# Block attention and a top-1 mixture of experts: k and q loaded one token a partition, one transposing transfer for each half

## The chip, the cores and the metric

The kernel runs on one core of a Trainium2 chip. The core has five engines, each with its own queue of instructions that it works off in order: PE (TensorE, the matrix multiplier, whose weight loads are listed apart as PEld), DVE (VectorE), ACT (ScalarE), POOL (GpSimd) and SP (SyncE, which here only issues transfers). Transfers run on 16 DMA engines. The metric is the device time of one execution in microseconds (us); lower is better.

## The reference

Eight batches of eight heads, 576 tokens each, 64 channels a head. Attention is causal by blocks of 64 tokens, and its output goes through a mixture of experts in which each token takes the one expert with the largest gate:

```python
scores = scale * np.matmul(q, k.transpose(0, 1, 3, 2))
mask = (pos[:, None] // 64) >= (pos[None, :] // 64)
scores = np.where(mask, scores, -1e9)
attn = np.exp(scores - scores.max(-1, keepdims=True))
attn = attn / (attn.sum(-1, keepdims=True) + 1e-9)
x = (attn @ v)                       # to (4608 tokens, 512)
logits = x @ w_gate                  # 8 experts
e_idx = np.argmax(logits, axis=1)
h = np.maximum(x[mask] @ w1[e], 0)   # 512 -> 1024, for the tokens of expert e
out[mask] = gate_w * sigmoid(x @ w_output_gate)[e] * (h @ w2[e])
```

Inputs and output are float32.

## The kernel before, in words

**Attention.** The 64 heads are taken two at a time: 32 pairs, each a `Pair` object. Products are made in 16-bit halves: a float32 operand is split into a high half (`ACT`, line 116) and the rest, a low half (`POOL`, line 117). For q and k both halves must stand with the 64 channels on the partitions, so they are turned. A pair goes through these steps:

- `fetch` (L104, L107) loads k and q of both heads into `nat`. The 576 tokens are one block of 64 (the "odd" block, L107) and four blocks of 128 (L104). In L104 partition p gets the four tokens 4p to 4p+3, which lie together in memory. Three `nat` buffers.
- `split` (L116, L117) writes the halves into `sp0` (high) and `sp1` (low), [128 partitions, 9 blocks, 128]. Two buffers of each.
- `turn` (L125, L127) is called once for `sp0` and once for `sp1`. Each time it issues five transposing transfers on SP: one of the odd block into `to`, and four of 32 partitions by 1024 columns into `tr`.
- `max_tile` (L165 to L197) multiplies q by k for the row maxima, `turn_max` (L206, L208) turns these, `prob_tile` (L222, L252) makes the products again, transposed, and takes the exponential on ACT into `pc` and `pcr`.
- `fetch_v`, `split_v` (L146, L150, L154, L155) load v with ten transfers into one of two buffers and split it. `values_odd` and `values` (L265 to L293) make the output, divide it and write it to `x_d` in memory with five transfers (L308, L311).
- `turn_x` and `finish_batch` (L318 and the lines from 475 on), after every fourth pair, make the gate of a batch and put its tokens into a table.

Since partition p holds tokens 4p to 4p+3, the order of tokens on the partitions is a mixed one (t, i), and v, the masks and `x_d` follow it: their patterns are "(i t) -> t i".

**Order of the work.** `round_of(g)` writes out the order of PE by hand: 139 rounds, four to a pair, in which several pairs are at different steps. Pair p takes its maxima in rounds 4p to 4p+2, its exponentials from 4p+5 on, its values in 4p+11 and 4p+12. The other engines get the order in which a scheduler places the same program's instructions; what has been placed on an engine is then worked off in that order. `turn` of pair p is written down at rounds 4p-7 and 4p-6, `split` at 4p-9 and 4p-8, `fetch` at 4p-12.

Products rotate through three PSUM buffers (`banks()`, `ps_s`): PE may fill one again when ACT or DVE have read it.

**Mixture of experts.** The last rounds overlap with the first tiles of the experts. After them come 22 steps; a step loads up to 4 MB of weights, splits them and multiplies (L763 to L924); each step's tokens are turned with one transposing transfer of 1024 or 2048 columns (`turned`, L854). The change leaves this part alone.

Of the kernel before, what the change touches and what calls it, by code (L numbers as in the profile page):

```python
# [8 lines left out]
F16 = mybir.dt.float16  # L9
# [5 lines left out]
ALU = mybir.AluOpType  # L15
# [5 lines left out]
P = 128  # L21
# [5 lines left out]
def block_attention_top1_moe(  # L27
# [11 lines left out]
    nc = tc.nc  # L39
    B, H, S, D = q.shape  # L40
# [5 lines left out]
    R0 = 64  # L46
# [3 lines left out]
    NR = 2 * S // P  # L50
    BIG = 60000.0
# [23 lines left out]
    sb = tc.alloc_tile_pool(name="sb", bufs=2)  # L75
# [16 lines left out]
    class Pair:  # L92


        def __init__(self, p):
            self.p = p
            self.b, self.hp = divmod(p, NP)
            self.tr, self.to = {}, {}

        def fetch(self):  # L100
            h0 = 2 * self.hp
            self.nat = ld.tile([P, 2, 2, 5, D], F32, name="nat", bufs=3)
            for w, src in enumerate((k, q)):
                nc.sync.dma_start(  # L104
                    self.nat[:, w, :, 1:5], src[self.b, h0:h0 + 2, R0:S].rearrange("h (p t) d -> p h t d", t=4)
                )
                nc.sync.dma_start(  # L107
                    self.nat[64 * w:64 * w + 64, 0, :, 0], src[self.b, h0:h0 + 2, 0:R0].rearrange("h p d -> p h d")
                )
            self.sp = [ld.tile([P, NR, P], F16, name=f"sp{c}", bufs=2) for c in range(2)]  # L110
# [6 lines left out]
                last_lo[0] = lo.tensor_tensor(sl[:, h], nat, sh[:, h], ALU.subtract)  # L117

        def room(self, c):
            self.tr[c] = sb.tile([P, 4, 2, P], F16, name=f"tr{c}", bufs=4)  # L120
            self.to[c] = sb.tile([P, P], F16, name=f"to{c}", bufs=4)

        def turn(self, c):
            self.room(c)
            nc.sync.dma_start_transpose(self.to[c], self.sp[c][:, 0])  # L125
            for n in range(4):
                nc.sync.dma_start_transpose(  # L127
                    self.tr[c][:, n].rearrange("c w (t i) -> c (w t) i", t=4),
                    self.sp[c][32 * n:32 * n + 32, 1:NR].rearrange("p r c -> p (r c)"),
                )  # L130

        def keys(self, c, ab, lo, hi):
            return self.tr[c][64 * ab:64 * ab + 64, lo:hi, 0]

        def asks(self, c, ab, lo, hi):
            return self.tr[c][64 * ab:64 * ab + 64, lo:hi, 1]

        def odd(self, c, ab, c0, c1):
            return self.to[c][64 * ab:64 * ab + 64, c0:c1]

        def fetch_v(self):
            h0 = 2 * self.hp
            self.vn, self.vh, self.vl = vns[self.p % 2], vhs[self.p % 2], vls[self.p % 2]
            for h in range(2):
                for n in range(4):
                    nc.sync.dma_start(  # L146
                        self.vn[:, 2 * n + h, 0:D],
                        v[self.b, h0 + h, R0 + P * n:R0 + P * n + P].rearrange("(i t) d -> t i d", t=4),
                    )
                nc.sync.dma_start(self.vn[64 * h:64 * h + 64, 8, 0:D], v[self.b, h0 + h, 0:R0])  # L150

        def split_v(self):
# [4 lines left out]
        def max_tile(self, i):  # L157
# [3 lines left out]
            def products(os, n, c0):  # L161
                m = P * (n + 1)
                main = [o[:, c0:c0 + m].rearrange("p (n x) -> p n x", x=P) for o in os]
                for ab in range(2):
                    nc.tensor.matmul(main[ab], self.asks(0, ab, n, n + 1)[:, 0], self.keys(0, ab, 0, n + 1), start=True, stop=False)  # L165
                for ab in range(2):
                    half = slice(64 * ab, 64 * ab + 64)
                    nc.tensor.matmul(  # L168
                        main[ab][:, n].rearrange("p (t i) -> p t i", t=4)[:, :, 16:32], mq[half], mk[half].rearrange("p (t x) -> p t x", t=4), start=False, stop=True
                    )  # L170
                for ab in range(2):
                    nc.tensor.matmul(
                        os[ab][:, c0 + m:c0 + m + R0], self.asks(0, ab, n, n + 1)[:, 0], self.odd(0, ab, 0, R0), start=True, stop=True
                    )

            if i < 2:
                ps = banks()
# [104 lines left out]
        def values(self, ab):  # L282
            for t in range(4):
                o = self.region(t)[:, ab]
                for c in range(t + 1):
                    i, c0 = ((1, 0), (0, 0), (2, 0), (0, 384))[c]
# [17 lines left out]
                self.xn.rearrange("p t (h d) -> p h t d", h=2), o[:, :, :, 0:D], sm.unsqueeze(3).broadcast_to([P, 2, NT, D]), ALU.mult  # L304
            )
            to = x_d[self.b * S:(self.b + 1) * S, self.hp * P:(self.hp + 1) * P]
            for n in range(4):
                nc.sync.dma_start(  # L308
                    to[R0 + P * n:R0 + P * n + P].rearrange("(i t) c -> t i c", t=4), self.xn[:, n]
                )  # L310
            nc.sync.dma_start(to[0:R0], self.xn[64:128, 4])  # L311

        def turn_x(self):
# [13 lines left out]
    with tc.high_priority(offset=3000):  # L327
# [12 lines left out]
        idg = const.tile([P, B, NT, 2], I32, name="idg")  # L340
# [13 lines left out]
    def masks():  # L354
# [10 lines left out]
        nc.vector.tensor_tensor(prt[:, 0:1], prt[:, 0:1], prt[:, 1:2], ALU.add)  # L365
        nc.vector.tensor_scalar(prt[:, 1:2], prt[:, 0:1], 31.5, -32.0, ALU.is_ge, ALU.mult)
        nc.vector.tensor_tensor(prt[:, 2:3], prt[:, 0:1], prt[:, 1:2], ALU.add)
        nc.vector.tensor_scalar(prt[:, 3:4], prt[:, 2:3], 15.5, BIG, ALU.is_le, ALU.mult)
        nc.vector.tensor_scalar(prt[:, 4:5], prt[:, 2:3], 15.5, None, ALU.is_ge)
        nc.vector.tensor_scalar(prt[:, 5:6], prt[:, 1:2], -1.0 / 16, None, ALU.mult)  # L370
        nc.vector.tensor_tensor(prt[:, 4:5], prt[:, 4:5], prt[:, 5:6], ALU.add)
        nc.vector.tensor_scalar(
            kext[:, 0:4], blk.unsqueeze(2).broadcast_to([P, 4, P]), prt[:, 4:5], -BIG, ALU.is_equal, ALU.mult
        )
        nc.vector.memset(kext[:, 0:4].rearrange("p n (t i) -> p n t i", t=4)[:, :, :, 0:16], 0.0)
        nc.vector.memset(kext[:, 4], 0.0)
        for a in (0, 64):
            nc.vector.memset(kext[a:a + 1], MS)
# [6 lines left out]
                )  # L385
        nc.gpsimd.memset(mk, BIG)
        nc.gpsimd.memset(mq, 0.0)
        nc.gpsimd.memset(mq.rearrange("p (t x) -> p t x", t=4)[:, :, 0:16], -BIG)

    def opening():  # L390


        x = Pair(0)
        y = Pair(1)
        x.fetch()
        y.fetch()
        x.split(0, nc.vector.tensor_copy, nc.vector)
        x.split(1, nc.scalar.copy, nc.gpsimd)
        rest = ps_v.tile([P, 2, 512], F32, name="ps_v")[:, 0].rearrange("p (a n) -> p a n", n=P)
        for i in range(2):  # L400
            x.room(i)
            ps = banks().rearrange("p a (b n) -> p (a b) n", n=P)
            for r in range(NR):
                nc.tensor.matmul(
                    ps[:, r - 1] if r else rest[:, i], x.sp[i][:, r], ident16, start=True, stop=True
                )
            to = x.tr[i].rearrange("c n w (t i) -> c w t n i", t=4)
            for w, cp in enumerate((nc.vector.tensor_copy, nc.scalar.copy)):
                for t in range(4):
                    cp(to[:, w, t], ps[:, 4 * w + t].rearrange("c (n i) -> c n i", n=4))  # L410
            nc.vector.tensor_copy(x.to[i], rest[:, i])
        y.split(0, nc.vector.tensor_copy, nc.gpsimd)
        y.split(1, nc.scalar.copy, nc.gpsimd)
        return x, y
# [4 lines left out]
    with tc.high_priority(offset=1000):  # L419
# [19 lines left out]
        nc.vector.tensor_scalar(t64, tcol, 64.0, None, ALU.mult)  # L439


        for t in range(4):
            nc.gpsimd.iota(idg[32 * t:32 * t + 32, :, 0:4, 0], pattern=[[S, B], [P, 4]], base=R0 + t, channel_multiplier=4)
        nc.gpsimd.iota(idg[:, :, 4, 0], pattern=[[S, B]], base=-R0, channel_multiplier=1)


# [520 lines left out]
    for p in range(1, NPR):  # L967
        base = 4 * p
# [191 lines left out]
```

## Time and profile before

| what | value |
|---|---|
| median of 3 runs | 1238.41 us (1229.64 to 1240.27) |
| the profiled execution's own time | 1231.79 us |
| its span, first to last instruction | 1230.1 us |
| busy in the span: PE, DVE, ACT, POOL | 66%, 44%, 37%, 28% |
| mean granted clock of PE | 0.805 of full speed |
| transfers issued by SP for attention | 918 |

The span has two parts. Up to about 765 us the pairs run, at a granted clock that is mostly 0.66 to 0.74, with PE busy half of the time; from 800 us on PE is busy for 0.89 to 0.96 of the time and the clock is at 0.93 to 0.99. A row of the timeline gives the start and the duration of an instruction (of several alike: of the group), engine and line, operation, destination and source; in brackets the idle time of the engine before it and what ended it. SP's rows have the time in which its queue was held by the issue of a transfer, waits included; the transfer itself comes after.

### The profile page before, as it was taken

How to read it: one execution, taken by the hardware profiler on the slowest of the kernel's cores; microseconds unless marked ns; L12 is line 12 of the kernel's file. 1: busy time of each engine (PE TensorE's matmuls, PEld its weight loads, DVE VectorE, ACT ScalarE, POOL GpSimd, SP SyncE). 2: the span in 40 equal slices, each digit the busy share in tenths (PEclk: the TensorE clock that was granted, in tenths of full speed). 3: DMA queues.
4: the chain of work that ended last, by engine and by line, in shares of the span. 5: the costliest groups of instructions: out<-in, count | busy, mean ns of one | idle time of the engine just before them, and what ended most of it. 6: DMA issues, size and time to landing. Idle time of an engine off the chain costs nothing. (4 is left out here: it accounts for less than half of the span.)

```text
span 1230.1 us, 23287 instructions
## 1 busy us (share of the span) xinstructions
PE 814.0 (66%) x8912; PEld 576.6 (47%) x8912; DVE 544.8 (44%) x928; ACT 457.6 (37%) x706; POOL 338.9 (28%) x392
## 2 busy tenths in 40 slices
PE   2155346455536553555535658689899999999996
PEld 1143234333324442344323436466667667667763
DVE  6032323232323332333223336524867768667741
ACT  2122223222222222322223223431766767657632
POOL 5122112311311231132131331544542232232101
PEclk9866767676666767667676778879999999999998
DMA  4232222332322332232332222624697999998141
GB/s 115 61 78 73 67 72 69 74 78 75 69 75 67 81 80 70 67 66 70 83 67 68 57 53 52 191 49 157 200 305 240 306 314 317 268 261 194 48 164 37
DMA packets 234920, 148.80 MB, mean 121 GB/s; under 512 B 172240, under 2 KB 207088, under 8 KB 234800
## 3 DMA queue, kind: packets, MB, share of 16 engines
q1 hardware_dynamic: 226752, 127.93, 38.7%
q0 software_dynamic: 8048, 19.29, 5.2%
q8 instruction: 72, 1.18, 0.4%
q14 instruction: 48, 0.39, 0.1%
HBM read 126.03 MB, written 19.34 MB: 118 GB/s over the span
## 5 line engine op out<-in xcount | busy, mean ns | idle before, releaser
L165 PE MATMUL ps_s<-tr 64*128 64x384 f16 (+3 forms) x256 | 54.2, 351 | 263.1 <-ACT pc L252 236.7
L256 DVE TENSOR_TENSOR lpc<-pc 128x512 f16<-128x512 f32 (+1 forms) x64 | 49.7, 776 | 377.4 <-ACT pc L252 377.4
L117 POOL TENSOR_TENSOR sp<-nat,sp 128x320 f16<-128x320 f32 (+1 forms) x126 | 90.3, 745 | 446.8 <-DMA tr<-sp 328.8
L886 PEld LDWEIGHTS <-w1b 128*128 128x128 f16 (+1 forms) x2208 | 176.6, 98 | 28.4 <-issue 5.1
L886 PE MATMUL ps_s<-xt,w1b 128*128 128x256 f16 (+5 forms) x1920 | 176.0, 253 | 2.9 <-DVE w1b L765 1.2
L116 ACT CAST sp<-nat 128x256 f16<-128x256 f32 (+1 forms) x124 | 45.1, 427 | 337.1 <-DMA tr<-sp 240.2
L915 PE MATMUL ps_o<-w2b,hh 128*128 128x512 f16 (+1 forms) x560 | 166.6, 379 | 1.7 <-ACT hh L894 1.4
L765 DVE TENSOR_TENSOR w2b<-w2f,w2b 128x1024 bf16<-128x1024 f32 x80 | 92.6, 1219 | 91.3 <-ACT w2b L763 90.0
L168 PEld LDWEIGHTS <-mq 64*128 64x128 f16 x256 | 13.4, 101 | 246.0 <-issue 245.9
L190 DVE TENSOR_REDUCE nmx<-ps_s 128x2 f32<-128x896 f32 (+3 forms) x128 | 82.1, 682 | 73.5 <-PE ps_s L182 67.3
L293 PE MATMUL ps_v<-vn,pc 128*128 128x65 f32 x512 | 109.7, 332 | 0.0
L915 PE MATMUL ps_o<-w2b,hl 128*128 128x512 f16 x280 | 106.1, 379 | 0.1
L765 DVE TENSOR_TENSOR w1b<-w1f,w1b 128x1024 bf16<-128x1024 f32 x80 | 93.0, 1217 | 3.7 <-ACT w1b L763 3.4
L293 PEld LDWEIGHTS ps_v<-vn,pc 128*128 128x128 f32 x512 | 88.9, 231 | 4.0
L924 POOL DMA_INDIRECT out_dram<-ys,ids x38 | 46.0, 1212 | 158.4 <-ACT ys L923 94.1
L252 ACT ACTIVATE pc<-ps_s 128x1024 f32<-128x1024 f32 (+1 forms) x96 | 82.1, 875 | 17.7 <-PE ps_s L222 17.0
L915 PEld LDWEIGHTS <-hh 128*128 128x128 f16 x560 | 54.2, 98 | 63.3 <-ACT hh L894 1.5
L763 ACT CAST w1b<-w1f 128x1024 f16<-128x1024 f32 x80 | 78.3, 1046 | 5.3 <-DMA w1f<-in_moe_w_dram 5.3
L763 ACT CAST w2b<-w2f 128x1024 f16<-128x1024 f32 x80 | 77.5, 1043 | 0.0
L222 PE MATMUL ps_s<-tr 64*128 64x384 f16 (+3 forms) x256 | 43.9, 337 | 42.4 <-ACT qe L208 18.3
L222 PE MATMUL ps_s<-tr,tr 64*128 64x512 f16 (+3 forms) x512 | 67.8, 344 | 3.9 <-issue 3.7
L318 PE MATMUL ps_s<-ident,xn 128*128 128x128 f32 x160 | 39.8, 410 | 45.2 <-ACT pc L252 42.2
(214 smaller groups left out, 1613.4 us busy)
## 6 DMA issues: line engine op xcount, KB each, us to landing
w1f<-in_moe_w_dram SPq DMA_DIRECT2D x80, 512.0 KB
w2f<-in_moe_w_dram SPq DMA_DIRECT2D x80, 512.0 KB
nat<-in_k_dram SPq DMA_DIRECT2D x32, 256.0 KB
nat<-in_q_dram SPq DMA_DIRECT2D x32, 256.0 KB
vn<-in_v_dram SPq DMA_DIRECT2D x256, 32.0 KB
x_d<-xn SPq DMA_DIRECT2D x128, 64.0 KB
tr<-sp SPq DMA_TRANSPOSE x248
hh<-in_moe_w_dram SPq DMA_DIRECT2D x4, 512.0 KB
```

The lines of the kernel that those rows point to most:

```text
L117: last_lo[0] = lo.tensor_tensor(sl[:, h], nat, sh[:, h], ALU.subtract)
L165: nc.tensor.matmul(main[ab], self.asks(0, ab, n, n + 1)[:, 0], self.keys(0, ab, 0, n + 1), start=True, stop=False)
L190: last_max[0] = nc.vector.tensor_reduce(self.nmx[:, t, :], ps[:, :, c0:c1], AX.X, ALU.max, negate=True)
L222: nc.tensor.matmul(os[ab], ks(kc, ab), qs(qc, ab), start=j == 0, stop=j == 3)
L252: last_exp[0] = nc.scalar.activation(self.pt[i], ap, AF.Exp, scale=SCALE)
L256: eng.tensor_tensor(self.pl[i][:, ab], self.pt[i][:, ab], self.high(i)[:, ab], ALU.subtract)
L293: nc.tensor.matmul(o, part(self.pt[1]), self.vn[:, ab], start=False, stop=False)
L763: nc.scalar.copy(hi, src)
L765: eng.tensor_tensor(lo[at], src[at], hi[at], ALU.subtract)
L886: nc.tensor.matmul(ph[:, f4].rearrange("p (h n) -> p h n", n=w), wv[:, cc, f, :], xv[:, cc], start=(k == 0), stop=(k == 3 * KD - 1))
L915: nc.tensor.matmul(py, hv[:, f, h], wv[:, f, :], start=(k == 0), stop=(k == 3 * KF - 1))
L924: nc.gpsimd.indirect_dma_start(out=out, out_offset=IOA(ap=ids[i][0:w, h, 0:1].bitcast(U32), axis=0), in_=ys[0:w], in_offset=None, bounds_c ...
```

## The change

`fetch` loads block by block, one token on each partition, with two transfers a tensor in place of one (one a head); the odd blocks stay. The tokens now stand in their own order, so one transposing transfer turns all nine blocks of a half, and `to` becomes block 0 of `tr`. v is loaded with one transfer a head in place of four, and `x_d` is written with one in place of four. The masks, the identity of a token (`idg`) and the copies of the first pair follow the new order.

```diff
         def fetch(self):
...
             for w, src in enumerate((k, q)):
-                nc.sync.dma_start(
-                    self.nat[:, w, :, 1:5], src[self.b, h0:h0 + 2, R0:S].rearrange("h (p t) d -> p h t d", t=4)
-                )
+                for h in range(2):
+                    nc.sync.dma_start(
+                        self.nat[:, w, h, 1:5], src[self.b, h0 + h, R0:S].rearrange("(t p) d -> p t d", p=P)
+                    )
                 nc.sync.dma_start(
                     self.nat[64 * w:64 * w + 64, 0, :, 0], src[self.b, h0:h0 + 2, 0:R0].rearrange("h p d -> p h d")
                 )
...
         def room(self, c):
-            self.tr[c] = sb.tile([P, 4, 2, P], F16, name=f"tr{c}", bufs=4)
-            self.to[c] = sb.tile([P, P], F16, name=f"to{c}", bufs=4)
+            self.tr[c] = sb.tile([P, NR, P], F16, name=f"tr{c}", bufs=4)
 
         def turn(self, c):
             self.room(c)
-            nc.sync.dma_start_transpose(self.to[c], self.sp[c][:, 0])
-            for n in range(4):
-                nc.sync.dma_start_transpose(
-                    self.tr[c][:, n].rearrange("c w (t i) -> c (w t) i", t=4),
-                    self.sp[c][32 * n:32 * n + 32, 1:NR].rearrange("p r c -> p (r c)"),
-                )
+            nc.sync.dma_start_transpose(self.tr[c], self.sp[c].rearrange("p r c -> p (r c)"))
 
         def keys(self, c, ab, lo, hi):
-            return self.tr[c][64 * ab:64 * ab + 64, lo:hi, 0]
+            return self.tr[c][64 * ab:64 * ab + 64, 1 + lo:1 + hi]
 
         def asks(self, c, ab, lo, hi):
-            return self.tr[c][64 * ab:64 * ab + 64, lo:hi, 1]
+            return self.tr[c][64 * ab:64 * ab + 64, 5 + lo:5 + hi]
 
         def odd(self, c, ab, c0, c1):
-            return self.to[c][64 * ab:64 * ab + 64, c0:c1]
+            return self.tr[c][64 * ab:64 * ab + 64, 0, c0:c1]
 
         def fetch_v(self):
...
             for h in range(2):
-                for n in range(4):
-                    nc.sync.dma_start(
-                        self.vn[:, 2 * n + h, 0:D],
-                        v[self.b, h0 + h, R0 + P * n:R0 + P * n + P].rearrange("(i t) d -> t i d", t=4),
-                    )
+                nc.sync.dma_start(self.vn[:, h:8:2, 0:D], v[self.b, h0 + h, R0:S].rearrange("(n p) d -> p n d", p=P))
                 nc.sync.dma_start(self.vn[64 * h:64 * h + 64, 8, 0:D], v[self.b, h0 + h, 0:R0])
...
                     nc.tensor.matmul(
-                        main[ab][:, n].rearrange("p (t i) -> p t i", t=4)[:, :, 16:32], mq[half], mk[half].rearrange("p (t x) -> p t x", t=4), start=False, stop=True
+                        main[ab][:, n, 64:P], mq[half], mk[half], start=False, stop=True
                     )
...
             to = x_d[self.b * S:(self.b + 1) * S, self.hp * P:(self.hp + 1) * P]
-            for n in range(4):
-                nc.sync.dma_start(
-                    to[R0 + P * n:R0 + P * n + P].rearrange("(i t) c -> t i c", t=4), self.xn[:, n]
-                )
+            nc.sync.dma_start(to[R0:S].rearrange("(n p) c -> p n c", p=P), self.xn[:, 0:4])
             nc.sync.dma_start(to[0:R0], self.xn[64:128, 4])
...
     def opening():
...
-            to = x.tr[i].rearrange("c n w (t i) -> c w t n i", t=4)
-            for w, cp in enumerate((nc.vector.tensor_copy, nc.scalar.copy)):
-                for t in range(4):
-                    cp(to[:, w, t], ps[:, 4 * w + t].rearrange("c (n i) -> c n i", n=4))
-            nc.vector.tensor_copy(x.to[i], rest[:, i])
+            tr = x.tr[i]
+            nc.vector.tensor_copy(tr[:, 1:5], ps[:, 0:4])
+            nc.scalar.copy(tr[:, 5:9], ps[:, 4:8])
+            nc.vector.tensor_copy(tr[:, 0], rest[:, i])
```

SP's queue in the middle of attention, one pair's worth, before the change. The names are the destination and the source of a transfer; the number behind x counts equal ones in a row. The loads of k and q around the turned pair's transfers are those of the pair four further on:

```order
L107 DMA nat<-in_q_dram 64x2x64
L127 DMA_TRANSPOSE tr_4455<-sp_4129 128x8x32 x2
L125 DMA_TRANSPOSE to_4456<-sp_4129 128x128
L127 DMA_TRANSPOSE tr_4455<-sp_4129 128x8x32 x2
L125 DMA_TRANSPOSE to_4515<-sp_4130 128x128
L127 DMA_TRANSPOSE tr_4514<-sp_4130 128x8x32
L146 DMA vn_98<-in_v_dram 128x1x64
L127 DMA_TRANSPOSE tr_4514<-sp_4130 128x8x32 x3
L146 DMA vn_98<-in_v_dram 128x1x64
L308 DMA x_d<-xn 4x32x128 x4
L311 DMA x_d<-xn 64x128
```

The same place in the queue of the changed kernel:

```order
L108 DMA nat<-in_q_dram 64x2x64
L140 DMA vn_98<-in_v_dram 128x4x64
L125 DMA_TRANSPOSE tr_3652<-sp_3329 128x9x128
L140 DMA vn_98<-in_v_dram 128x4x64
L125 DMA_TRANSPOSE tr_3700<-sp_3330 128x9x128
L298 DMA x_d<-xn 128x4x128
L299 DMA x_d<-xn 64x128
L141 DMA vn_98<-in_v_dram 64x64 x2
L105 DMA nat<-in_k_dram 128x4x64 x2
L108 DMA nat<-in_k_dram 64x2x64
```

Ten transposing transfers of a pair have become two, of 128 by 9 by 128 elements, and each now stands behind one load of v.

ACT's queue before the change, from the last exponential of one round to the next ones (`sp` is the high half, `vh` that of v, `pc` an exponential's result):

```order
L252 ACTIVATE pcr<-ps_s 128x576
L154 CAST vh_100<-vn_98 128x7x64
L116 CAST sp_5193<-nat 128x5x64 x2
L116 CAST sp_5193<-nat 128x4x64 x2
```

And with the change:

```order
L243 ACTIVATE pcr<-ps_s 128x576
L117 CAST sp_5091<-nat 128x5x64 x2
L117 CAST sp_5091<-nat 128x4x64
L145 CAST vh_101<-vn_99 128x7x64
L243 ACTIVATE pc_4937<-ps_s 128x1024
L117 CAST sp_5091<-nat 128x4x64
L243 ACTIVATE pc_4938<-ps_s 128x1024
```

The four casts of the split stood together behind the one of v; now three stand ahead of it and one between two exponentials.

## Rows read from the trace of the kernel before

**Rows 1.** The page: span; busy time, share and instructions of engines.

```profile
span 1230.1 us, 23287 instructions
PE 814.0 (66%) x8912; PEld 576.6 (47%) x8912; DVE 544.8 (44%) x928; ACT 457.6 (37%) x706; POOL 338.9 (28%) x392
```

**Rows 2.** Who waited for whom, 100 to 765 us: total, times, longest, us.

```profile
ACT sp L116 <- DMA tr<-sp: 240.2, 22, 13.6
...
PE ps_s L165 <- ACT pc L252: 228.9, 22, 14.4
```

**Rows 3.** SP's timeline over one pair, 634 to 659 us.

```profile
634.04 0.53 SPq L104 DMA_DIRECT2D nat<-in_k_dram  x1
...
637.36 3.82 SPq L127 DMA_TRANSPOSE tr<-sp  x3
641.27 1.17 SPq L125 DMA_TRANSPOSE to<-sp  x1
...
656.19 1.69 SPq L146 DMA_DIRECT2D vn<-in_v_dram  x3
...
658.53 0.53 SPq L104 DMA_DIRECT2D nat<-in_k_dram  x1
```

**Rows 4.** Lines by tile: count, ns min/median/max, first and last start us.

```profile
L127 SPq DMA_TRANSPOSE tr<-sp x248: 1174/1250/2317, 11.3 to 764.4; - x124
...
L104 SPq DMA_DIRECT2D nat<-in_k_dram x32: 418/572/3817, 0.9 to 658.5; - x32
L107 SPq DMA_DIRECT2D nat<-in_k_dram x32: 612/660/1526, 1.4 to 659.1; - x32
...
L146 SPq DMA_DIRECT2D vn<-in_v_dram x256: 73/549/2222, 47.6 to 798.5; - x128
L150 SPq DMA_DIRECT2D vn<-in_v_dram x64: 507/513/684, 50.1 to 789.6; - x64
...
L308 SPq DMA_DIRECT2D x_d<-xn x128: 503/536/1342, 106.1 to 823.4; - x128
...
L854 SPq DMA_TRANSPOSE xt<-xr x20: 1242/3460/8732, 865.3 to 1165.2; - x20
...
L165 PE MATMUL ps_s<-tr x256: 215/333/606, 12.8 to 786.3; 64*128 64x384 f16 x32, 64*128 64x256 f16 x32, 64*128 64x128 f16 x32, 64*128 64x512 f16 x32
```

**Rows 5.** PE's timeline, the product that waits once a pair.

```profile
647.75 0.58 PE L165 MATMUL ps_s<-tr 64*128 64x512 f16 x1 [12.01 <-ACT pc L252]
...
659.47 0.37 PE L165 MATMUL ps_s<-tr 64*128 64x512 f16 x1 [0.56 <-DVE nmx L190]
671.73 0.58 PE L165 MATMUL ps_s<-tr 64*128 64x512 f16 x1 [11.88 <-ACT pc L252]
```

**Rows 6.** Stretches: length; PE, PEld, DVE, ACT, POOL busy; PE clock; DMA share, GB/s.

```profile
100.00:600.00 500.00, 247.62 (x3200) 178.01 (x3201) 156.73 (x327) 127.73 (x243) 112.94 (x133) 0.67 0.31 73
...
647.70:651.70 4.00, 3.72 (x48) 2.64 (x47) 2.30 (x4) 2.21 (x5) 0.00 (x0) 0.50 0.24 55
651.70:659.90 8.20, 7.59 (x122) 5.59 (x119) 5.14 (x9) 1.91 (x3) 5.07 (x6) 1.00 0.28 67
```

**Rows 7.** ACT's timeline, the casts of the split.

```profile
645.36 1.43 ACT L116 CAST sp<-nat 128x320 f16<-128x320 f32 x4 [12.02 <-DMA tr<-sp]
```

**Rows 8.** SP's timeline, two transposing transfers of the second part.

```profile
927.21 1.26 SPq L854 DMA_TRANSPOSE xt<-xr  x1
...
1039.67 3.21 SPq L756 DMA_DIRECT2D w2f<-in_moe_w_dram  x4
1043.41 8.73 SPq L854 DMA_TRANSPOSE xt<-xr  x1
```

**Rows 9.** DMA, 928.2 to 930 us: busy tenths in 40 slices; packets.

```profile
DMA  0000157999999999999999999852000000000022
...
DMA packets 1060, 0.26 MB, mean 146 GB/s; under 512 B 1060, under 2 KB 1060, under 8 KB 1060
```

**Rows 10.** The same view, 629 to 634 us, while v is loaded.

```profile
DMA  2232222222322246768223223333432111232201
...
DMA packets 1048, 0.40 MB, mean 80 GB/s; under 512 B 540, under 2 KB 1047, under 8 KB 1047
```

More of the change, by code (lines that the diff above doesn't have):

```diff
@@ L97, in __init__ @@
             self.b, self.hp = divmod(p, NP)
-            self.tr, self.to = {}, {}
+            self.tr = {}
         def fetch(self):
@@ L367, in masks @@
         nc.vector.tensor_tensor(prt[:, 2:3], prt[:, 0:1], prt[:, 1:2], ALU.add)
-        nc.vector.tensor_scalar(prt[:, 3:4], prt[:, 2:3], 15.5, BIG, ALU.is_le, ALU.mult)
+        nc.vector.tensor_scalar(prt[:, 3:4], prt_i, 63.5, BIG, ALU.is_le, ALU.mult)
         nc.vector.tensor_scalar(prt[:, 4:5], prt[:, 2:3], 15.5, None, ALU.is_ge)
@@ L374, in masks @@
         )
-        nc.vector.memset(kext[:, 0:4].rearrange("p n (t i) -> p n t i", t=4)[:, :, :, 0:16], 0.0)
+        nc.vector.memset(kext[:, 0:4, 0:64], 0.0)
         nc.vector.memset(kext[:, 4], 0.0)
@@ L387, in masks @@
         nc.gpsimd.memset(mq, 0.0)
-        nc.gpsimd.memset(mq.rearrange("p (t x) -> p t x", t=4)[:, :, 0:16], -BIG)
+        nc.gpsimd.memset(mq[:, 0:64], -BIG)
     def opening():
@@ L439, in block_attention_top1_moe @@
         nc.vector.tensor_scalar(t64, tcol, 64.0, None, ALU.mult)
-        for t in range(4):
-            nc.gpsimd.iota(idg[32 * t:32 * t + 32, :, 0:4, 0], pattern=[[S, B], [P, 4]], base=R0 + t, channel_multiplier=4)
+        nc.gpsimd.iota(idg[:, :, 0:4, 0], pattern=[[S, B], [P, 4]], base=R0, channel_multiplier=1)
         nc.gpsimd.iota(idg[:, :, 4, 0], pattern=[[S, B]], base=-R0, channel_multiplier=1)
```

## The prediction

> **What bounds the kernel now.** Begin with the page: in a span of 1230 us the busiest engine, PE, works 66% and no other half [rows 1]. So most of the loss is waiting, and the view of waits says where: between 100 and 765 us ACT stands 240 us in front of the casts that split k and q, 22 times, up to 13.6 us each, until a transposing transfer is through; PE stands 229 us, also 22 times, for an exponential of ACT [rows 2]. These are one wait. ACT's queue has the casts ahead of that exponential, the casts need a free `sp` buffer, and it becomes free when the transfers that turn the pair two before have read it. On the timelines ACT waits 12.02 us, does four casts in 1.43 us [rows 7], and 1 us later PE goes on after 12.01 us [rows 5].
>
> Why are the transfers late? SP's timeline has no gap: from one pair's first load to the next one's it is 24.5 us, filled with issues back to back [rows 3]. Over all pairs, from the first product of maxima at 12.8 us to the last at 786.3, it is 773.5/31 = 24.95 us a pair [rows 4]. So **SP's queue sets the pace**: 29 issues a pair, and an issue costs about the same whatever it carries.
>
> **The change on SP.** Medians are from rows 4. Taken away from a pair: eight transposing transfers of 32 partitions (1.25 us) and two of the odd block (1.17 us [rows 3]), 12.3 us; six of eight loads of v (0.55 us), 3.3 us; three of four writes of `x_d` (0.54 us), 1.6 us. Added: two more loads of k and q, 1.1 us by the 0.57 us of today's, though each now has 512 pieces of 256 bytes in place of 256 of 1 KB. A load of v, with 128 pieces, costs the same 0.55, so I see no price per piece.
>
> The two merged transposing transfers are the open price: no row shows 128 by 1152. The nearest is the 1024-column one of the second part, which turns 0.26 MB [rows 9] and holds SP for 1.26 us with an idle queue ahead [rows 8]; the small one, with a quarter of that, takes 1.25. Hence 1.27 each is what I take. Bounds: 1.2 from below; from above 8.73, the longest `xt` issue, which stood right behind 2 MB of weights [rows 8]; in between, 3.46, the median of `xt` [rows 4], and 5.6, if the 1.25 us grew with the bytes (288 KB for 64).
>
> SP's sum per pair: 2 x 1.27 + 4 x 0.57 + 2 x 0.66 + 2 x 0.55 + 2 x 0.51 (odd v) + 0.54 + 0.51 (`x_d`, the last priced as odd v) = 9.3 us, and 14 gaps of some 0.06 us: **10.2 us** in place of 24.5.
>
> **What is late next.** PE. Between two of its stalls it runs 12.1 us (647.75 to 659.84, the first start of rows 5 and the end of the second) with the same products as after the change, and nearly without a gap. Four of these, right behind its 12 us of idling, are at clock 0.50, the level of 1.2 GHz, and 8.2 at 1.00, 2.4 GHz [rows 5, 6]. Without the stall it doesn't idle like that, and I expect the level of 2.4 GHz throughout. The 4.0 us then take between 2.0 (all of it PE's) and 4.0 (none), and I take 2.6, since DVE and ACT, busy 2.3 and 2.2 us of it, don't get faster. That gives 10.8 us; the gate of a batch, after every fourth pair, adds some 0.4 when spread, and 0.3 goes to a split cast that now stands between two exponentials (0.36 us, a quarter of the 1.43 [rows 7]). **11.5 us a pair**, with SP close behind at 10.2.
>
> The cover for the rest: per pair, at 24.95 us, DVE is busy 156.73/500 x 24.95 = 7.8 us, ACT 6.4, POOL 5.6 [rows 6]; each fits in 11.5. If POOL falls behind in the pair with five table writes, SP's loads wait for its split (a `nat` buffer), and a load of v and the next transposing transfers stand behind them. These are wanted only when the split two pairs on begins, about a pair's length after the issue, so this should pass. The new order of SP also puts one load of v ahead of each transposing transfer; it waits for PE's values of the pair two before, four rounds ahead of the use, and I price it at nothing, since four rounds (11.5 us) cover two loads and two issues (3.6 us) and the transfer (1.1 us [rows 9]). The masks cost the same number of products. In the opening, two more loads stand before pair 0's q is complete (+1.2 us), eight small copies become two, and the first turned pairs arrive behind more loads: together +4 us. The experts' part is untouched.
>
> **Sum.** 1231.8 (the profiled execution, 0.5% below the median of 1238.4) - 31 x (24.95 - 11.5) + 4 = 1231.8 - 417 + 4 = 819 us; I say **820**. My case holds from 10.2 us a pair (779) to 14.6 (915), the latter being the 12.1 us of a stretch whose clock does not rise, plus casts and one exponential in line (2.5).
>
> **Rivals.**
> - *The DMA engines become the bound* (0.13). Pieces of 1 KB become 256 bytes. While v and `x_d` are moved today the engines deliver only 80 GB/s [rows 10]. A pair moves 0.59 MB of k and q, 0.29 of v, 0.29 of `x_d`; at 80 GB/s that is 14.6 us, and two turned halves of 0.29 MB at 1.1 us per 0.26 (24 busy slices of 0.045 us [rows 9]) are 2.4, less what goes side by side: some 16 us a pair, 958 us. Against it: in rows 10 the busy share is mostly 2 to 3 tenths, so the engines had room and were not fed evenly. The Trainium skill, "DMA: Bandwidth & Descriptors", section Specifications, speaks against the change: full rate needs pieces of 512 bytes or more, below which the engine reads, modifies and writes. The busy share of rows 10 doesn't yet show such a limit. The same page, section on why a DMA increments its semaphore by 16, says that the slowest dimension of both patterns picks the number of engines: by that a pattern that starts with t = 4 runs on four of 16, the new ones on all. The 2 to 3 tenths of rows 10 agree, and by it this rival would weigh less.
> - *SP stays the bound, because a merged issue costs by its size* (0.12). At 5.6 us each a pair takes SP 11.2 + 7.7 = 18.9 us, 1048 us; at 3.46 us 14.6, 915. For it: the spread of `xt`. Against: the 1.26 us at 927 us.
> - *Slower: a merged transfer's issue is held until the loads queued ahead have drained* (0.03), as at 1043 us. Place: both transposing transfers behind six loads of 0.59 MB. At 8.73 each: 17.5 + 7.7 = 25.2 us, 1231.8 + 31 x 0.25 + 4 = 1244. It decides from (24.95 - 7.7)/2 = 8.6 us an issue. Against: today's transposing transfers stand behind the same bytes of k and q, and their median is 1.25.
> - *No change, 1232 us* (0.03): the casts wait for the landing of the last transposing transfer and not for the queue, and the landing stays as late. Against: SP's queue without a gap.
>
> My forecast has 0.66; 0.03 is left for what I don't see.
>
> **How the numbers follow.** The predicted time is my forecast's. The range, 772 to 960, takes in nearly all of that case, the DMA rival and the cheap end of the SP rival: about 0.8. Three runs of before differ by 0.9%, so 1% is about what can be told from no change. Faster by over 1%: 0.66 + 0.13 + 0.12 and most of the unseen = 0.93; within: 0.03; slower: 0.04.
>
> **What would show it.** Right: SP's timeline has two transposing issues of 1.2 to 1.4 us a pair, and gaps; ACT's wait for them falls from 240 us to under 30; PE is busy over 85% at a clock above 0.9 during attention; products of maxima end near 370 us. Wrong: transposing issues of 3 us or more (SP rival), a DMA share over 0.8 with SP waiting (DMA rival), PE's clock back at 0.50 within the pairs, or a new wait of ACT's casts for loads of k and q.

## The result, and the profile after

The changed kernel takes **983.87 us** (median of 4 runs, 973.59 to 991.47) where the kernel before takes 1234.84 beside it: a ratio of 0.794 (95% interval 0.786 to 0.802). Medians here are of all runs, while ratios leave out those over 1.5% above the fastest of their kernel. The forecast was 820, range 772 to 960: the direction was right, and the forecast 164 us too low.

The page of the profiled execution (982.18 us) has a span 250 us shorter, and PE at 84% in place of 66% [rows 1]:

```profile
span 980.2 us, 22497 instructions
...
PE 820.9 (84%) x8893; PEld 586.8 (60%) x8912; DVE 567.9 (58%) x922; ACT 456.7 (47%) x700; POOL 349.9 (36%) x389
```

The next rows group instructions by tile (count, minimum, median and maximum in ns, first and last start), and answer to [rows 4]. L156 is the old L165:

```profile
L156 PE MATMUL ps_s<-tr x256: 217/332/631, 10.6 to 531.7; 64*128 64x384 f16 x32, 64*128 64x256 f16 x32, 64*128 64x128 f16 x32, 64*128 64x512 f16 x32
...
L125 SPq DMA_TRANSPOSE tr<-sp x62: 1252/1332/3103, 12.1 to 498.0; - x62
```

A merged transposing issue costs 1.33 us, against 1.27 forecast. The products of maxima run from 10.6 to 531.7 us, so T, the time of a pair, is 521.1/31 = **16.81 us** where 11.5 was forecast. 31 x 5.31 = 165 us, which is nearly the whole error: the tail behind the last of them is 4.7 us longer than it was (980.2 - 531.7 = 448.5 us; before, 1230.1 - 786.3 = 443.8), and the start 2.2 us shorter.

SP's timeline over a pair has gaps now, against [rows 3]; there are 14 issues a pair:

```profile
319.85 0.54 SPq L140 DMA_DIRECT2D vn<-in_v_dram  x1
323.15 1.33 SPq L125 DMA_TRANSPOSE tr<-sp  x1
324.57 0.53 SPq L140 DMA_DIRECT2D vn<-in_v_dram  x1
325.15 1.52 SPq L125 DMA_TRANSPOSE tr<-sp  x1
326.77 0.53 SPq L298 DMA_DIRECT2D x_d<-xn  x1
327.35 0.50 SPq L299 DMA_DIRECT2D x_d<-xn  x1
329.19 1.12 SPq L141 DMA_DIRECT2D vn<-in_v_dram  x2
332.43 0.92 SPq L105 DMA_DIRECT2D nat<-in_k_dram  x2
```

It issues nothing from 320.39 to 323.15, nor from 330.31 to 332.43. SP's queue now waits itself, for POOL's split and for PE (total, times, longest, in us, between 100 and 500 us; before, no line of this view has more than 5.7 us from 100 to 765):

```profile
SPq L105 <- POOL sp L118: 43.8, 16, 4.7
SPq L141 <- POOL vl L146: 42.2, 20, 6.0
SPq L125 <- PE ps_s L213: 40.9, 18, 3.4
```

Who waited for whom among the engines in the same stretch, to be held against [rows 2]:

```profile
POOL vl L146 <- ACT vh L145: 130.1, 14, 13.4
...
ACT sp L117 <- DMA tr<-sp: 64.6, 20, 4.9
...
PE ps_s L156 <- ACT pc L243: 42.1, 22, 3.9
...
PE ps_s L306 <- ACT pc L243: 15.0, 22, 1.6
...
PE ps_s L213 <- DVE nmx L188: 10.8, 6, 3.0
```

The wait of ACT's casts for a transposing transfer is smaller and has not gone: it was to fall under 30 us. ACT's timeline shows what it does:

```profile
323.20 0.65 ACT L243 ACTIVATE pcr<-ps_s 128x576 f32<-128x576 f32 x1 [0.80 <-PE ps_s L213]
326.11 1.12 ACT L117 CAST sp<-nat 128x320 f16<-128x320 f32 x3 [2.26 <-DMA tr<-sp]
327.40 0.56 ACT L145 CAST vh<-vn 128x448 f16<-128x448 f32 x1 [0.17 <-DMA vn<-in_v_dram]
327.88 0.40 ACT L117 CAST sp<-nat 128x256 f16<-128x256 f32 x1
328.18 1.01 ACT L243 ACTIVATE pc<-ps_s 128x1024 f32<-128x1024 f32 x1
```

The next exponential, at 328.18, the first of the pair behind, stands after five casts, and the first cast stands 2.26 us until the transfer issued at 323.15 has read its `sp`. That transfer goes out 0.05 us before the exponential `pcr` starts: PE's last scores of the pair four before, just done, free its `tr` buffer. So, as I read these rows, each pair runs once round a loop: PE's scores, the transfer, the casts, the next exponential, PE.

What it does to the clock (stretches; columns as in [rows 6]):

```profile
325.50:331.10 5.60, 3.57 (x47) 1.91 (x44) 5.41 (x12) 3.95 (x8) 3.00 (x4) 1.00 0.59 132
331.10:333.20 2.10, 0.00 (x0) 0.00 (x0) 2.10 (x9) 0.64 (x3) 2.10 (x3) 0.63 0.04 8
333.20:341.50 8.30, 8.26 (x100) 6.65 (x99) 3.54 (x11) 1.44 (x4) 0.61 (x2) 0.50 0.39 89
341.50:345.00 3.50, 3.50 (x60) 2.89 (x62) 1.72 (x4) 0.65 (x1) 2.89 (x3) 0.94 0.79 118
```

PE works in pieces up to 331, idles 2.1 us, in which the clock falls, and then works without a gap for 8.3 us at 0.50, the level of 1.2 GHz. Over 100 to 500 us:

```profile
100.00:500.00 400.00, 310.43 (x3928) 225.81 (x3925) 207.97 (x415) 146.85 (x280) 145.04 (x159) 0.74 0.51 99
```

In T's 16.8 us PE is busy 13.0 and idle 3.8, at a mean clock of 0.74.

### The profile page after: what moved, and what is told of

It is laid out like the page before. It is cut to its first block, busy times and chain, and to the rows that moved or that the text cites. A ratio compares the mean times of both kernels' runs of the same rounds, so it can differ in the third digit from the quotient of the medians.

```text
span 980.2 us, 22497 instructions
## 1 busy us (share of the span) xinstructions
PE 820.9 (84%) x8893; PEld 586.8 (60%) x8912; DVE 567.9 (58%) x922; ACT 456.7 (47%) x700; POOL 349.9 (36%) x389
## 5 line engine op out<-in xcount | busy, mean ns | idle before, releaser
L156 PE MATMUL ps_s<-tr 64*128 64x384 f16 (+3 forms) x256 | 53.1, 346 | 78.7 <-ACT pc L243 47.5
L284 PE MATMUL ps_v<-vn,pc 128*128 128x65 f32 x512 | 116.8, 348 | 0.0
L146 POOL TENSOR_TENSOR vl<-vn,vh 128x448 f16<-128x448 f32 x32 | 33.2, 1037 | 226.0 <-ACT vh L145 174.8
L118 POOL TENSOR_TENSOR sp<-nat,sp 128x256 f16<-128x256 f32 (+1 forms) x126 | 100.2, 815 | 30.2 <-ACT sp L117 26.2
L247 DVE TENSOR_TENSOR lpc<-pc 128x512 f16<-128x512 f32 (+1 forms) x64 | 53.5, 836 | 98.9 <-ACT pc L243 98.8
L910 POOL DMA_INDIRECT out_dram<-ys,ids x38 | 50.0, 1317 | 155.2 <-ACT ys L909 91.0
L213 PE MATMUL ps_s<-tr,tr 64*128 64x384 f16 (+5 forms) x768 | 98.5, 340 | 0.0
L284 PEld LDWEIGHTS ps_v<-vn,pc 128*128 128x128 f32 x512 | 94.9, 246 | 4.3
L213 PEld LDWEIGHTS <-tr 64*128 64x128 f16 (+1 forms) x1152 | 53.1, 110 | 67.6 <-issue 40.1
L213 PE MATMUL ps_s<-tr 64*128 64x256 f16 (+5 forms) x384 | 66.4, 341 | 26.6 <-DVE nmx L188 14.4
```

What stands on the lines that cost most here:

```text
L213: nc.tensor.matmul(os[ab], ks(kc, ab), qs(qc, ab), start=j == 0, stop=j == 3)
L247: eng.tensor_tensor(self.pl[i][:, ab], self.pt[i][:, ab], self.high(i)[:, ab], ALU.subtract)
L284: nc.tensor.matmul(o, part(self.pt[1]), self.vn[:, ab], start=False, stop=False)
L910: nc.gpsimd.indirect_dma_start(out=out, out_offset=IOA(ap=ids[i][0:w, h, 0:1].bitcast(U32), axis=0), in_=ys[0:w], in_offset=None, bounds_c ...
```

## The experiments

T is read in every run from the first and the last product of maxima. It is 24.95 us before and 16.81 in the changed kernel. Each T comes from one profiled execution, and the four runs of the changed kernel lie 18 us apart, which is at most 0.6 us a pair; a smaller difference in T is not clear of noise by itself. Line numbers differ by one or two between kernels.

**1. Does SP's number of issues, or their size, still count?** `four_v_x` loads v and writes `x_d` in four transfers each again, in the new order of tokens (9 more issues a pair); `five_turns` turns each half in five transfers:

```diff
-                nc.sync.dma_start(self.vn[:, h:8:2, 0:D], v[...].rearrange("(n p) d -> p n d", p=P))
+                for n in range(4):
+                    nc.sync.dma_start(self.vn[:, 2 * n + h, 0:D], v[self.b, h0 + h, R0 + P * n:R0 + P * n + P])
```

```diff
-            nc.sync.dma_start_transpose(self.tr[c], self.sp[c].rearrange("p r c -> p (r c)"))
+            for r0, r1 in ((0, 1), (1, 3), (3, 5), (5, 7), (7, 9)):
+                nc.sync.dma_start_transpose(self.tr[c][:, r0:r1], self.sp[c][:, r0:r1].rearrange("p r c -> p (r c)"))
```

> v and x_d again in four transfers a block, in the tokens' own order: nine more issues on SP a pair (29 - 15 + 9 = 23 a pair with ten transposing ones still merged into two). In the order that the scheduler makes of it the casts stand behind the exponentials. Theory: SP's sum is 9.3 + 9 x 0.55 us and gaps of 0.06, about 15 us a pair, and the wait in ACT's queue is gone; 15 to 16 us a pair, 984 - 31 x (0.8 to 1.8) = 928 to 960 us, faster with more issues. Rival (issues set the pace): 984 + 31 x 9 x 0.6 = 1150 us.

> Each half is turned in five transfers (1, 2, 2, 2, 2 blocks) in place of one; all else, and the order on all engines, as in the changed kernel. Theory (the casts wait for the end of the five of the high half, behind PE): 4 x 1.25 = 5.0 us more in the chain each pair, and SP's sum 9.3 + 8 x 1.25 + gaps = 20.5 us; 22 to 24 us a pair, 984 + 31 x (5 to 7) = 1139 to 1200 us. Rival (only SP's sum counts): 20.5 us a pair, 1099 us. Rival (neither, the DMA engines or the clock hold the kernel): below 1050 us.

`five_turns`: 1189.61 us (one run), T 23.41. Its transposing transfers, of 32 to 64 KB in place of 288, cost as much each:

```profile
L126 SPq DMA_TRANSPOSE tr<-sp x310: 1128/1243/3769, 10.8 to 708.0; - x155
```

So a transposing issue of 32 to 288 KB has about one price, and merging the ten into two is worth 206 of the 251 us. T lies above SP's sum of 20.5 us, as the theory of a chain had it. `four_v_x`: 962.79 us (ratio 0.778, 0.772 to 0.784), T 16.04. It is *faster* than the change, with 9 more issues, so SP's number of issues doesn't set the pace in the changed kernel. On ACT's timeline of `four_v_x` between 290 and 322 us no long exponential stands behind a cast that waits, which I take for the reason; this run doesn't test it alone. At 23 issues SP's queue is full again, without a gap over 0.1 us between 289.90 and 323.32 us, so 16.04 is about what SP needs there:

```profile
302.45 0.50 SPq L301 DMA_DIRECT2D x_d<-xn  x1
303.06 1.33 SPq L125 DMA_TRANSPOSE tr<-sp  x1
304.44 3.44 SPq L141 DMA_DIRECT2D vn<-in_v_dram  x4
307.92 0.49 SPq L142 DMA_DIRECT2D vn<-in_v_dram  x1
```

**2. A fifth `tr` buffer** (`bufs=5`), since the transfer waits for one:

> Five buffers of turned halves in place of four. The scheduler uses it to place casts and transposing transfers one pair earlier, and the transfer behind the load of v still needs the buffer that the same products of PE free. Theory: the same wait, 984 us within 1.5%. Rival (the turned buffers are too few): the stall goes, 795 to 897 us.

980.77 us (one run), T 16.60. The program's scheduler moves the transfers and casts a pair ahead, and the wait of ACT's casts for a transposing transfer is nearly as long as it was (57.4 us from 100 to 500, for 64.6).

**3. The split's casts behind the exponential** (`late_casts`):

```diff
-                hi(sh[:, h], nat)
+                with tc.issue_after(last_exp[0].ins) if last_exp[0] else nullcontext():
+                    hi(sh[:, h], nat)
```

> Only the place of the high-half casts in ACT's queue changes: each is placed behind the latest exponential written so far, so that it needs a transposing transfer of the pair before and not the one just issued. Theory (the casts wait for a transposing transfer that itself waits for PE, and the next exponential stands behind them): PE's 2.8 us a pair behind exponentials go, and if the clock then stays at 1.00, PE's 13.0 busy us a pair shrink to about 10; 10.7 to 14.0 us a pair in place of 16.8, so 984 - 31 x (2.8 to 6.1) = 795 to 897 us. Rival (PE is slow because its clock does not hold, whatever the wait): 960 to 990 us, granted clock still near 0.75. Rival (the number of issues on SP still sets the pace): 984 us, since none is taken away.

963.86 us (ratio 0.783, 0.778 to 0.787), T 16.11: most of the gain did not come, and the time fell into the range of the rival that blames the clock (0.76 from 100 to 400). The casts of k and q no longer wait for a transposing transfer, but now the cast of v waits for its load (58.8 us from 100 to 500), with the two long exponentials behind it (ACT's timeline):

```profile
239.82 0.56 ACT L146 CAST vh<-vn 128x448 f16<-128x448 f32 x1 [6.26 <-DMA vn<-in_v_dram]
240.29 1.02 ACT L244 ACTIVATE pc<-ps_s 128x1024 f32<-128x1024 f32 x1
```

**4. Is it the clock?** `warm` gives PE ten products a pair that nobody reads, at the places where it waits, so that its clock stays up; `warm_late` does so on `late_casts`:

```diff
+            w = ps_v.tile([P, 2, 512], F32, name="ps_v")
+            for _ in range(n):
+                nc.tensor.matmul(w[:, 0], ident16, kext[:, 0:4].rearrange("p n x -> p (n x)"), start=True, stop=True)
```

> The changed kernel with ten more products a pair on PE that nothing reads (identity by the key mask, 128 by 512, into the value bank while it is free): two ahead of each half of the third max_tile product, two ahead of turn_x, four ahead of the third prob_tile, the places where PE idles for a short time behind ACT and DVE. 2.1 us of work more at 2.4 GHz. Theory (the short idle gaps, 3.8 us a pair, make the clock fall to 0.50, and PE then works some 8 us at that level; 13.0 busy us a pair in place of 9.8): filled gaps keep the clock at 1.00; 9.8 + 2.1 + 1.7 = 13.6 us a pair, 984 - 31 x 3.2 = 885 us (850 to 930), faster with more work. Rival (the waits alone set the time and the clock only follows): 975 to 1000 us. Rival (PE's work sets the time): 984 + 31 x 2.1 to 4.2 = 1049 to 1114 us.

> The same ten products in the kernel whose casts stand behind the exponentials (963.9 us). Theory of the clock: clock at 1.00 in most of attention, PE 9.8 + 2.1 us and gaps left of 1 to 2 us; 13 to 14 us a pair, 865 to 900 us. If only the waits count: 955 to 980 us. If PE's work counts: 1030 us and more.

`warm`: 959.72 us (ratio 0.775, 0.770 to 0.779), T 16.12; `warm_late`: 958.74 us (0.774, 0.769 to 0.779), T 15.85. The clock did go up, from 0.74 to 0.92 in `warm` (100 to 500 us):

```profile
100.00:500.00 400.00, 337.79 (x4456) 213.05 (x4455) 221.88 (x443) 157.27 (x297) 147.44 (x166) 0.92 0.50 101
```

The time fell by 24 us against the changed kernel, a seventh of what was missed, and by 5 against `late_casts`; 959.72 lies between the ranges of the clock theory and of the rival of the waits, and fits neither. The ten products are work too, some 2.1 us a pair at 2.4 GHz by the expectation, and what of them lay in the loop was not measured: 24 us is the clock's gain less their price. So this run alone doesn't tell how much of the loss is the clock's own. With 18 products (978.06 us, one run) the kernel is slower than with ten, and ten on `four_v_x`, whose SP queue is full, make that one slower (981.04).

**5. The gate left out.** The distances between the copies `qe`, one a pair, showed a pattern in `late_casts`: 11.8, 16.1, 19.1, 18.0 us in one batch and much the same in the others, with the long ones around the gate of a batch. `after_no_gate` and `late_no_gate` leave `finish_batch` out for batches 0 to 6, with fixed counts in its place; the experts' part differs then, so only T is read.

```diff
-                later.append(finish_batch(self.b, xT))
+                if self.b == B - 1:
+                    later.append(finish_batch(self.b, xT))
+                else:
+                    nc.vector.memset(run_cnt[:, self.b + 1, :], S / E / P * (self.b + 1))
```

> The changed kernel without the gate of batches 0 to 6: finish_batch (its products, its some twenty small operations on VectorE, its five table writes on GpSimd) runs for the last batch alone, and a single fill of run_cnt stands in its place, so the routing and the later part differ; what is read is T, the time from the first to the last product of maxima over 31 (16.8 us in the changed kernel), and the distances between the copies qe, pair by pair. Theory (the batch's gate, which the forecast priced at 0.4 us a pair, is the larger part of what was missed: the pairs around it took 19 to 20 us beside 12 in the kernel with late casts): T falls to 12.5 to 13.5, and the pattern of four is gone. Rival (the casts' wait for the transposing transfer and the clock that falls after it): T stays at 15.8 to 16.8, all pairs alike.

> The kernel with late casts (T 16.05 us, pairs of 11.9, 16.1, 20.4, 19.4) without the gate of batches 0 to 6, left out as in the run beside it. Theory of the gate: every pair at 11.5 to 13, T 12 to 13. Rival (waits for loads and the clock): T 14.5 to 16.

T is 15.49 on the changed kernel (1.32 less) and 14.24 on `late_casts` (1.87 less). The first comes nearer to the rival's 15.8 than to the theory's 13.5; the second, 14.24, lies under the rival's range and above the theory's. The gate costs something, and is not the larger part.

**6. All casts behind the exponentials** (`late_all`): on top of `late_casts`,

```diff
-            nc.scalar.copy(self.vh[:, sl, 0:D], self.vn[:, sl, 0:D])
+            with tc.issue_after(last_exp[0].ins) if last_exp[0] else nullcontext():
+                nc.scalar.copy(self.vh[:, sl, 0:D], self.vn[:, sl, 0:D])
```

`late_v` has this edit without that of `late_casts`, and `late_all_no_gate` both without the gate.

> The kernel with late casts, and the cast of v too behind the exponential that was issued last, so that ScalarE has none of its three exponentials behind a wait for a load or a transposing transfer (it waited 58.8 us for v's load in 400 us, 2.4 us a pair); the gate as it is. Theory of the waits: T 13.5 to 14.5, 875 to 915 us. Rival (the gate sets the pace): T 15.5 to 16.1, 945 to 966 us.

> The changed kernel with only the cast of v behind the exponential issued last; the casts of k and q stay where the changed kernel has them, ahead of the exponentials, where the first of them waits for the transposing transfer (56 us in 330). With the two kernels at hand (casts of k and q late: T 16.0 us a pair; all late: 13.3; none: 16.8) this is the fourth corner. Theory (ScalarE's queue in order: an exponential is as late as the last transfer that any cast ahead of it waits for, so taking one of two waits away gains little): T 16.0 to 16.8, 955 to 985 us. Rival (v's load alone is what cost): T 13.3 to 14.3, 875 to 905 us.

> Both: all casts behind the exponentials, and no gate of batches 0 to 6. If the gate and ScalarE's waits are together what the forecast of 11.5 us a pair missed: T 11.5 to 12.2 with the clock above 0.9 in the middle. If something else holds the pairs (the queue of transfers, GpSimd): T above 13.

`late_all` takes **875.56 us** (ratio 0.704, 0.698 to 0.710), T 13.27, the best here along with `late_spread` and `late_apart` of number 8. `late_v` takes 971.15 (two runs), T 16.34; its ACT waits longer for the transposing transfers than the changed kernel's did (56.2 us from 100 to 430 there):

```profile
ACT sp L117 <- DMA tr<-sp: 83.4, 18, 8.6
```

Late casts of k and q alone give 0.7 us a pair, of v alone 0.5, which are hardly clear of noise, both together **3.5**. ACT's queue is as late as the last transfer that a cast in it waits for, so one of two waits taken away hands its time to the other. In `late_all` the exponentials stand first (ACT's timeline of a pair without a gate):

```profile
248.47 1.94 ACT L245 ACTIVATE pc<-ps_s 128x1024 f32<-128x1024 f32 x2 [2.28 <-DVE xn L296]
250.30 0.82 ACT L118 CAST sp<-nat 128x320 f16<-128x320 f32 x2
...
252.94 0.59 ACT L147 CAST vh<-vn 128x448 f16<-128x448 f32 x1
```

and PE, with the same products, has a higher clock from 100 to 400 us than in the changed kernel (0.73 there):

```profile
100.00:400.00 300.00, 244.52 (x3839) 183.73 (x3839) 191.16 (x404) 146.30 (x285) 149.70 (x162) 0.89 0.71 131
```

A pair has 10.8 us of PE busy and 2.5 idle, for 13.0 and 3.8: of the 3.5 us, 2.2 are products that run faster and 1.3 are idle time. No work was added to PE for it, so the low clock of the changed kernel was in large part a consequence of the waits.

The quickest pairs without a gate take 10.1 us at the full clock, less than the forecast's 11.5, though the mean without any gate is 11.71, as the next run shows (four pairs in a row, columns as in [rows 6]; the first has no gate, the next two have its parts):

```profile
244.10:254.20 10.10, 9.33 (x170) 7.12 (x170) 7.41 (x13) 6.25 (x12) 5.55 (x7) 1.00 0.88 163
254.20:268.20 14.00, 11.11 (x193) 8.27 (x191) 10.20 (x29) 7.37 (x15) 5.17 (x7) 1.00 0.69 152
268.20:284.60 16.40, 13.10 (x171) 9.87 (x170) 8.37 (x17) 6.47 (x13) 11.33 (x13) 0.75 0.75 117
284.60:295.80 11.20, 10.41 (x172) 7.46 (x170) 7.41 (x13) 6.29 (x13) 4.48 (x5) 0.91 0.83 145
```

`late_all_no_gate`: T 11.71, from its line of products of maxima, and the stretch from 100 to 340 us:

```profile
L158 PE MATMUL ps_s<-tr x256: 215/332/607, 10.7 to 373.8; 64*128 64x384 f16 x32, 64*128 64x256 f16 x32, 64*128 64x128 f16 x32, 64*128 64x512 f16 x32
```

```profile
100.00:340.00 240.00, 204.27 (x3398) 156.81 (x3394) 151.95 (x268) 127.55 (x244) 110.05 (x121) 0.94 0.79 155
```

PE is busy 85% at a clock of 0.94, and the last product of maxima starts at 373.8: the picture that the prediction drew (over 85%, above 0.9, near 370).

**7. The same order of casts in the kernel before** (`before_late`):

> The kernel before (its 29 issues a pair, its 5 transposing transfers of each half) with all casts behind the exponential issued last, as in the 875 us kernel. Theory (before, SP's 24.5 us of issues a pair set the pace, and the order on ScalarE only decides who is seen to wait): T 24.3 to 25.2, 1215 to 1240 us. Rival (the casts' place was the bound all along, and the change itself was not needed): T below 22, under 1140 us.

1245.02 us (ratio 1.009, 1.006 to 1.012), T 25.26, a little over the theory's end. There SP's queue did set the pace, and the casts' place was worth nothing. The order of the casts gives its further 0.887 (0.704/0.794) only behind the change.

**8. Which part of the gate?** On `late_all`: `late_all_no_scatter` leaves the five table writes of batches 0 to 6 out; `late_spread` has three rounds between them instead of one; `late_apart` also puts each behind a subtraction of the split on POOL:

```diff
-        for t in range(NT):
+        for t in range(NT if b == B - 1 else 0):
```

```diff
-            sc = nc.gpsimd.indirect_dma_start(
+            with tc.issue_after(last_lo[0].ins):
+                sc = nc.gpsimd.indirect_dma_start(
...
-            yield
+            for _ in range(3 if b < B - 1 else 1):
+                yield
```

> The 875 us kernel (all casts late) without the five table writes of batches 0 to 6; the rest of the gate stays, and the routing's counts with it. The table then lacks those tokens, so the later part gathers fewer rows; T and the pairs are read. Of the gate's 11 us a batch (pairs of 14.0 and 16.8 beside two of 10.1): theory that GpSimd's five writes of 1.28 us, which stand ahead of its subtractions, are the longer pair: 14.0 stays and 16.8 falls to 10 to 11.5, T 11.9 to 12.4. Rival (the clock or VectorE's small operations carry over into the next pair): 16.8 stays above 14, T above 12.8.

> The 875 us kernel with the five table writes three rounds apart instead of one, in batches 0 to 6, so that they stand over four pairs and not in one. Theory that five writes in a row hold GpSimd's subtractions back: the pair of 16.8 falls to about 12, the others rise by 0.5 to 1 each, T 12.3 to 12.9, 845 to 865 us. Rival (each write costs its 1.28 us wherever it stands, or the pair is long for another reason): T 13.2 to 13.6, 868 to 885 us.

> The 875 us kernel with the five table writes of each of batches 0 to 6 really apart: each is put behind the subtraction of the split issued last on GpSimd, three rounds from one to the next, so that a pair has one or two of them; in the kernel before this one they still stood in a row (214.56 to 221.16 us). Theory, from the run without the writes (pair of 10.3 in place of 16.8, T 12.1): five writes in a row hold back GpSimd's subtraction of the lows, for which ScalarE's exponential and VectorE then wait; apart, T 12.2 to 12.9 and 835 to 862 us. Rival (each write costs its 1.28 us wherever it stands, or its transfer does): T 13.2 to 13.6, 868 to 885 us.

Without the writes T is 12.22, so they cost 1.05 us a pair of the gate's 1.56 (13.27 - 11.71), and the pair of 16.4 us is gone. Three pairs in a row, the second and third with the parts of the gate:

```profile
177.60:187.70 10.10, 9.33 (x170) 7.14 (x170) 7.41 (x13) 6.24 (x13) 5.56 (x7) 1.00 0.74 167
187.70:201.70 14.00, 11.10 (x195) 8.28 (x189) 10.21 (x29) 7.36 (x16) 5.16 (x7) 1.00 0.63 143
201.70:212.00 10.30, 9.52 (x173) 7.23 (x172) 8.27 (x17) 6.28 (x13) 5.53 (x7) 1.00 0.72 161
```

`late_spread`: 871.28 us (0.702 to 0.712), T 13.22, and no test: on POOL's timeline the writes still stand in a row, since the scheduler was free to put them there.

```profile
214.56 0.99 POOL L536 DMA_INDIRECT tab_d<-idg,sli  x1 [3.14 <-DVE sli L520]
215.85 1.48 POOL L536 DMA_INDIRECT tab_d<-idg,sli  x1 [0.30 <-issue]
```

`late_apart` does move them apart:

```profile
223.99 0.97 POOL L537 DMA_INDIRECT tab_d<-idg,sli  x1 [0.30 <-issue]
...
231.50 0.98 POOL L537 DMA_INDIRECT tab_d<-idg,sli  x1 [0.16 <-issue]
...
241.63 0.98 POOL L537 DMA_INDIRECT tab_d<-idg,sli  x1 [0.16 <-issue]
```

and takes 875.27 us (0.702 to 0.715), T 13.53: nothing gained, as the rival had it. My theory of the row of writes fell. That the writes cost some 1.05 us a pair is shown, by one execution each; by what way, POOL's time or their transfers among the others, stays open. One place can be seen in `late_all`: once a batch an exponential of ACT stands until within 2 us of the end of the row of writes, 26.7 us in five batches from 100 to 400, for something that the view can't name ("remote"):

```profile
ACT pc L245 <- remote: 26.7, 5, 7.8
```

This wait is gone in `late_all_no_scatter`, and in `late_apart` too, where T didn't fall; so it isn't the whole way.

## Why the prediction was wrong, and where it was right

- **What bounds before: right.** SP's queue of 29 issues set the pace. `before_late` shows that the place of ACT's casts did not, and `five_turns`, with the issues of transposing transfers back, is back at 23.41 us a pair, though there by way of the loop and not by SP's sum alone (20.5).
- **The price of a merged issue: right**, 1.33 us against 1.27 taken, and far from the ends of 3.46 and 8.73. So the rivals "SP stays the bound" and "slower" fall. SP has gaps, as said.
- **The DMA engines as the bound (958 us): no,** though the measured time lies near it. From 100 to 500 us they are busy 0.51 at 99 GB/s, and in the quickest pair of `late_all` they deliver 163 GB/s. The 80 of [rows 10] was no limit.
- **The tail: right** within 5 us. The opening was to cost 4 us more; the first product of maxima came 2.2 us earlier.
- **The step that failed is "What is late next": 11.5 us a pair.** With ACT's waits and the gate taken away it is 11.71, where the forecast without its 0.4 for the gate was 11.1. The 5.31 us come in three pieces:
  - *3.5 us, priced at nothing: ACT's queue.* I wrote that the transposing transfers, and v's load ahead of them, are wanted about a pair's length after the issue, so a delay should pass. But ACT takes its queue in order, and the casts that want those transfers stand ahead of the exponentials that PE wants at once. What the casts can spare, the exponentials behind them can't. With 24.95 us a pair I could see this wait [rows 2, 7] and took it for a mere effect of SP; it is also a loop of its own (PE, transfer, cast, exponential, PE), which takes over as soon as SP is quick. `late_all` shows the size, 16.81 to 13.27; the corners `late_casts` and `late_v` show that either wait alone keeps most of it. That the transfer in turn waits for PE is read from SP's waits (40.9 us) and was not taken away by an experiment.
  - *1.2 us: the gate of a batch, 1.6 in place of 0.4.* 13.27 to 11.71, two thirds of it the table writes. The 0.4 is about what the gate's products take of PE (11.11 - 9.33 = 1.8 us a batch in the rows of `late_all`); the writes' 1.05 was priced at nothing. "It should pass" was said of POOL in that pair, and it didn't: SP's loads wait 43.8 us for POOL's split between 100 and 500. That the stall of 12 us a pair hid all this in the kernel before is likely, and no run shows it.
  - *0.6 us* that I don't assign, no more than the noise of T.

  31 x (3.5 + 1.2 + 0.6) = 164 us. Taken in the other order the whole gate comes to 1.3 and the casts to 3.8.
- **The clock: the forecast of 2.4 GHz throughout was wrong as it stood (0.74), in large part by consequence.** With the casts' waits gone it rises by itself, to 0.89, and to 1.00 in quiet pairs. Held at 0.92 with unread products the time falls by 24 us, with their own price in it. The upper end of my case, 14.6 us a pair, was to stand for a clock that does not rise, but its 12.1 us hold only 4.0 at 0.50 and 8.2 at 1.00; in the changed kernel one pair has 8.3 at 0.50.

## What to carry to other kernels

When a bound is lifted, look not only at the next busiest engine but at each in-order queue: what stands in it ahead of the instruction that the critical engine waits for, and which transfers that waits for in turn. An operation that has time to spare hasn't any if an urgent one stands behind it; put the urgent one first, and do so for all the waits of that queue at once, since one alone gains nearly nothing. A stall that is seen at one place before the change can be a loop of its own, and rare work (a gate every fourth pair) needs a price on every queue that it enters.

## What the runs showed of the hardware

- In the pair shown PE's clock fell from 1.00 to 0.50 within a pause of 2.1 us (331.1 to 333.2), behind 5.6 us in which PE was busy 3.57, and stayed at 0.50 for 8.3 us of work without a gap. In the kernel before, after 12 us of idling, it was back at 1.00 after 4.0 us of work [rows 6]. So the longer pause was not the dearer one here; the runs don't show why.
- A transposing issue takes SP 1.24 us (median) for 32 to 64 KB and 1.33 for 288 KB.
- The DMA engines were busy 0.31 for 73 GB/s before [rows 6], 0.51 for 99 in the changed kernel and 0.88 for 163 in the quickest pair of `late_all`: 21 and 27% more time per byte. The Trainium skill, "DMA: Bandwidth & Descriptors", section Specifications, puts full rate at pieces of 512 bytes or more, and k and q now move in pieces of 256. The direction agrees, but the size isn't theirs alone: `five_turns` has the same pieces and is busy 0.36 for 80 GB/s from 100 to 500 us, 6% more than before. In the changed kernel, at 0.51, it was no bound.
